# Windowed attention and two expert layers on one core: all filling matmuls ahead of the first scores, two more behind them, and a plan that books a slow start

## The chip, the cores and the metric

One core of a Trainium2 chip runs the whole program in one launch. The metric is device time in microseconds (us), the median of three runs. The engines are named as in the profile: PE is TensorE (PEld its weight loads), DVE is VectorE, ACT is ScalarE, POOL is GpSimd, SP is SyncE, which issues most DMAs.

## The reference

Attention over 4 batches and 8 heads, with 512 local and 32 global positions of 64 numbers each. A local query sees the 32 global keys and the local keys within 32 positions; a global query sees all keys. Two expert layers follow, on 2304 tokens of 512 numbers.

```python
# attention, per batch and head
out_g = softmax(scale * q_g @ k_all.T) @ v_all                    # 32 global queries
s_l   = concat([scale * q_l @ k_g.T, where(|i-j| <= 32, scale * q_l @ k_l.T, -1e9)])
out_l = softmax(s_l) @ concat([v_g, v_l])                         # 512 local queries
x = concat([out_g, out_l]) -> (2304, 512)
# first expert layer
h = x @ w_in                      # 512 -> 2048
x = (h * clip(h + 3, 0, 6) / 6) @ w_out
# second expert layer
h = maximum(maximum(x @ w1, x @ w2), x @ w3)    # 512 -> 768
return h @ w_out2
```

## The kernel before

**Stages.** Attention runs in 16 steps, one for each pair of heads of a batch (`pair`, line 440), with a step for the global queries of two pairs each (`globals_`, line 555). Beside it the first product of the first expert layer (`first`, line 680, matmuls of line 694) starts as soon as a batch of tokens and a decoded piece of `w_in` are there. The other products follow: the long one (line 858), the second layer's (line 982).

**One pair.** Its queries (`qr`), keys (`kr`) and values (`vr`) come by DMA from SP (lines 451, 454); each has three slots, so the load of a fourth pair waits until the first pair's slot is free. PE makes the scores (line 468, 64 small matmuls into two PSUM banks). DVE masks them and takes the row maxima (line 481), ACT the exponentials (line 487). PE turns the result over, once for each of the two heads (`flip`, line 511, four transposes each); DVE or ACT copies it out of PSUM (line 434, `pt<-s`); PE multiplies by the values (line 522), DVE norms (line 530), PE turns that over (line 537), ACT and DVE store it in two parts (lines 549 and 551). The global queries of two pairs have their own scores (line 575, twelve matmuls) and product with the values (line 619), which is the last reader of both pairs' values.

**The filling matmuls.** `fill` (line 417) writes a whole PSUM bank from a tile of ones, a matmul of 128 by 512. There are seven banks in which scores lie during the first pairs: five named `s`, and `bank` 6 and 7. Scores leave some columns unwritten, and the filling gives those a value. Before, six fillings stand ahead of the first scores, and the seventh (the fifth `s` bank) behind the first half of the first pair's scores. The first pair's scores are split in halves, since its queries and keys come in two loads each (the keys' by ACT's queue).

**What sets the order.** Every step is handed to a planner (`Plan.order`, line 141) with its engine, a booked duration, a due number and what it reads and writes. It walks through time by its own bookkeeping and gives each engine a fixed order of instructions. On the chip each engine then runs its list in that order, waiting where an input is not there yet. Booked durations steer only this order. For PE the planner also books twice the duration for 4 us behind a long idle time (`cold`, lines 234 to 237), and waits for the loading of PE's own instructions, 256 at a time (`border`). It begins as if PE were at full pace. A step with `rel` isn't taken up before that time; a smaller due number goes first.

Of the kernel before, what the change touches and what calls it, by code (L numbers as in the profile page):

```python
# [99 lines left out]
class Plan:  # L100
# [40 lines left out]
    def order(self):  # L141
# [4 lines left out]
        free, cand, out, pipe, port, form = {}, {}, [], 0.0, dict(DVE=0.0, POOL=0.0), "F"  # L146
# [9 lines left out]
        self.stalls = []  # L156
        count, border, there, loads, cold = 0, FIRST, 0.0, [], -1e9

# [36 lines left out]
        while len(out) < len(self.ops):  # L195
# [34 lines left out]
            if o.eng == "PE":  # L230
                if FORM.get(o.what, "F") != form:
                    form = FORM.get(o.what, "F")
                    us += TURN
                if t - free.get("PE", 0.0) > 2.0 and t > COLD:
                    cold = t + 4.0
                if t < cold:
                    us += min(us, (cold - t) / 2)
                count += o.ni
                if count > border:
                    at_ = t + us * (1 - (count - border) / o.ni)  # L240
                    wait_ = max(0.0, there - at_)
                    at_, us = at_ + wait_, us + wait_
                    if wait_ > 0.2:
                        self.stalls.append((round(at_, 1), round(wait_, 1)))
                    if wait_ > 2.0:
                        cold = at_ + 4.0
                    behind = max([p - at_ for i, p in loads if i <= at_] + [0.0])
                    there, border = at_ + 3.2 + min(4.0, 0.45 * behind), border + 256
# [29 lines left out]
FIRST = 193  # L278
COLD = 6.0
SPLIT = 2  # L280
# [14 lines left out]
def body(ctx, tc, q_n, k_n, v_r, w_in, w_o, w_3, w_4, out):  # L295
    nc = tc.nc
# [126 lines left out]

    full = [filled(bank) for bank in (*sbanks[:4], banks[6], banks[7])]

# [14 lines left out]
    def pair(b, pr, s0):  # L440
# [7 lines left out]
        for n, (t, src, cut, size) in enumerate(((Q, q_n, 256, NQ + SG), (K, k_n, 448, NK))):  # L448
            for i, (a, z) in enumerate(((0, cut), (cut, size)) if first_ else ((0, size),)):
                e, issue = ("ACT", nc.scalar) if first_ and n else ("SP", nc.sync)  # L450
                op(e, 0.45, lambda t=t, src=src, a=a, z=z, issue=issue: issue.dma_start(
                    out=t()[:, a:z], in_=src[b, pr][:, a:z]), s0 - 6 + i, w=[(t, i)] if first_ else [t],
                   kb=(z - a) / 2, rel=s0 - 14, what="qk"[n])
        op("SP", 0.5, lambda: nc.sync.dma_start(out=V(), in_=v_r[b, pr]), s0 - 3 + 5 * first_, w=[V], kb=1024, rel=s0 - 10, what="v")

        TB, NM, OB = [Buf(T["t"]) for _ in range(2)], Buf(T["nm"]), Buf(T["o"])
        for u, tiles in enumerate(((0, 1), (2, 3)) if first_ else (range(4),)):
# [3 lines left out]
            def scores(tiles=tiles, SB=SB):  # L461

                for i in tiles:
                    for c in range(4):
# [10 lines left out]
                      w=SB + [(t, "held") for t in TB], what="scores", ni=32 * len(tiles))  # L475
            if not full[6:]:
                full.append(filled(sbanks[4], [head]))
            for n, (hh, i) in enumerate((hh, i) for hh in range(2) for i in tiles):
# [749 lines left out]
```

## Time and profile before

| | us |
|---|---|
| median of three runs (719.79 to 720.88) | 719.81 |
| the profiled execution's own time | 722.88 |
| its span in the trace | 721.1 |
| PE busy | 700.2 |
| DVE, ACT, POOL busy | 533.1, 377.2, 125.9 |
| DMA, mean over the span | 200 GB/s |

The profiled execution took 3.07 us longer than the median, 1.78 us of it outside the span. Busy time of PE counts a matmul from its start to a modelled end, so a busy PE is not always a PE at its peak: the same matmuls take longer where the engine's clock is lower. The granted clock in the profile's rows (PEclk) reads 1.00 where no record of a lower one is there, and at the very start there is no record; there the durations tell.

### The profile page before, as it was taken

The numbers are of one execution on the slowest core, as the hardware profiler recorded it, in microseconds if no ns is written. First come the engines' busy times: TensorE is split into PE (matmuls) and PEld (weight loads), VectorE is DVE, ScalarE is ACT, GpSimd is POOL, SyncE is SP. The second block draws the span as 40 slices with busy tenths as digits, with TensorE's granted clock in tenths as the row PEclk, the third lists the DMA queues.
The fourth block names the chain that finished last, engine by engine and source line by source line (L and its number), as shares of the span: only waits on it lengthen the run. The fifth ranks groups of instructions, "written<-read, shape, count | busy, mean of one in ns | idle before, by whom it ended". The sixth has DMA issues, their size and how long they took to land.

```text
span 721.1 us, 16051 instructions
## 1 busy us (share of the span) xinstructions
PE 700.2 (97%) x6380; PEld 619.7 (86%) x6380; DVE 533.1 (74%) x1123; ACT 377.2 (52%) x802; POOL 125.9 (17%) x160
## 2 busy tenths in 40 slices
PE   8899998999999999999999999999999999999998
PEld 5677776778878999988899888898999999998998
DVE  4898886667864476699976679898978876576781
ACT  5788776754332244456564366754444435154452
POOL 2125543210001142103000000021211220021210
PEclk9999999999999999999999999999999999999999
DMA  8869888726863775686576588101363471366452
GB/s 340 306 236 343 299 315 309 275 90 193 316 234 161 283 279 193 225 258 194 150 227 188 151 263 272 66 0 59 125 213 113 151 236 57 103 202 210 139 159 88
DMA packets 73147, 144.57 MB, mean 200 GB/s; under 512 B 4976, under 2 KB 43632, under 8 KB 70000
## 3 DMA queue, kind: packets, MB, share of 16 engines
q1 hardware_dynamic: 72784, 143.13, 58.5%
q8 instruction: 50, 0.82, 0.5%
q10 hardware_dynamic: 288, 0.41, 0.2%
q14 instruction: 25, 0.20, 0.1%
HBM read 98.04 MB, written 45.48 MB: 199 GB/s over the span
## 4 chain that ended last, share of the span: by engine, by line
PE 70%; DMA 13%; DVE 9%; ACT 4%; issue 2%; POOL 1%; SPq 1%; DVEq 0%; ACTq 0%; POOLq 0%
PE bank L982 30%; PE bank L858 20%; PE bank L694 16%; DMA raw<-in_w_o_dram 3%; DMA raw<-in_w_in_dram 2%; DMA kr<-in_kn_dram 2%; DMA raw<-in_w_dram 2%; DMA rf<-hd 2%; DMA hd<-rf 1%; ACT t L487 1%; PE s L468 1%; PE s L511 1%; DVE rq L651 1%; DMA gsA<-rq 1%; DVE rr L676 1%
## 5 line engine op out<-in xcount | busy, mean ns | idle before, releaser
L694 PE MATMUL bank<-rx,rw 128*128 128x512 f32 (+1 forms) x960 | 199.8, 364 | 1.7 <-issue 1.0
L694 PEld LDWEIGHTS bank<-rx,rw 128*128 128x128 f32 x960 | 162.8, 189 | 25.4 <-issue 2.4
L858 PE MATMUL bank<-rr,rw 128*128 128x320 f32 (+2 forms) x912 | 155.2, 331 | 2.1 <-DVE rr L676 1.2
L858 PEld LDWEIGHTS bank<-rr,rw 128*128 128x128 f32 x912 | 140.3, 188 | 16.4 <-DVE rr L676 2.2
L982 PE MATMUL bank<-rw,rr 128*128 128x256 f32 (+2 forms) x648 | 100.1, 302 | 0.6 <-DVE rf L438 0.5
L982 PEld LDWEIGHTS bank<-rw,rr 128*128 128x128 f32 x648 | 90.6, 188 | 5.7 <-ACT rf L434 0.7
L676 DVE TENSOR_TENSOR rr<-fw,rr 128x1024 fp32r<-128x1024 f32 (+2 forms) x76 | 73.5, 973 | 22.6 <-ACT rr L781 21.8
L781 ACT CAST rr<-fw 128x1024 fp32r<-128x1024 f32 (+2 forms) x76 | 61.9, 819 | 52.9 <-PE bank L858 46.0
L704 ACT ACTIVATE rq<-bank,three 128x512 f32<-128x512 f32 (+1 forms) x60 | 37.7, 633 | 49.1 <-PE bank L694 41.6
L676 POOL TENSOR_TENSOR rf<-rf 128x256 f32<-128x256 f32 (+2 forms) x34 | 33.5, 998 | 141.1 <-DVE rf L651 39.6
L434 ACT COPY rf<-bank 128x512 f32<-128x512 f32 (+2 forms) x71 | 32.5, 466 | 48.9 <-PE bank L982 39.4
L706 DVE SCALAR_TENSOR_TENSOR rq<-rq,bank 128x512 f32<-128x512 f32 (+1 forms) x60 | 36.9, 619 | 28.1 <-ACT rq L704 27.8
L982 PE MATMUL bank<-rw,re 128*128 128x256 f32 (+2 forms) x369 | 54.3, 292 | 1.5 <-DVE rf L996 0.8
L982 PE MATMUL bank<-re,rr 128*128 128x512 f32 x222 | 55.0, 391 | 0.0
L487 ACT ACTIVATE t<-t,nm 128x128 f32<-128x128 f32 x128 | 49.7, 392 | 9.0 <-DVE nm L481 9.0
L676 POOL TENSOR_TENSOR rq<-rq 128x256 f32<-128x256 f32 (+2 forms) x43 | 35.9, 835 | 97.1 <-DVE rq L676 85.3
L982 PEld LDWEIGHTS bank<-rw,re 128*128 128x128 f32 x369 | 49.4, 188 | 3.3 <-DVE rf L996 1.0
L982 PEld LDWEIGHTS bank<-re,rr 128*128 128x128 f32 x222 | 40.7, 188 | 7.9
L1076 DVE TENSOR_TENSOR rf<-rf,bank 128x320 f32<-128x320 f32 (+2 forms) x72 | 37.0, 529 | 13.7 <-PE bank L982 12.5
L676 DVE TENSOR_TENSOR rf<-rf 128x256 f32<-128x256 f32 (+4 forms) x54 | 29.3, 573 | 7.0 <-DMA rf<-hd 6.8
L481 DVE CUSTOM_DVE_ANT_0 t<-s,mask 128x128 f32<-128x128 f32 x116 | 26.6, 285 | 9.4 <-PE s L468 9.4
L676 DVE TENSOR_TENSOR re<-rf,re 128x1024 fp32r<-128x1024 f32 (+4 forms) x20 | 26.5, 1331 | 3.5 <-ACT re L1159 3.5
(134 smaller groups left out, 970.4 us busy)
## 6 DMA issues: line engine op xcount, KB each, us to landing
vr<-in_v_dram SPq DMA_DIRECT2D x16, 1024.0 KB, 8.2
fw<-gsB SPq DMA_DIRECT2D x28, 512.0 KB, 4.5
raw<-in_w_dram SPq DMA_DIRECT2D x24, 512.0 KB, 4.2
fw<-gsC SPq DMA_DIRECT2D x28, 320.0 KB, 3.5
raw<-in_w_in_dram SPq DMA_DIRECT2D x16, 512.0 KB, 7.9
raw<-in_w_o_dram SPq DMA_DIRECT2D x16, 512.0 KB, 4.3
fw<-gsA SPq DMA_DIRECT2D x28, 256.0 KB, 2.8
gsB<-rq SPq DMA_DIRECT2D x6, 1024.0 KB, 4.6
```

The lines of the kernel that those rows point to most:

```text
L434: (nc.scalar.copy if eng == "ACT" else nc.vector.tensor_copy)(out=out, in_=in_)
L468: nc.tensor.matmul(SB[hh]()[QB * c:QB * c + QB, 128 * i + a:128 * i + z], lhsT=Q()[64 * hh:64 * hh + 64, QB * j:QB * j + QB], rhs=K()[64 * ...
L481: nc.vector.tensor_tensor_reduce(out=TB[hh]()[:, i], in0=SB[hh]()[:, 128 * i:128 * i + 128], in1=mask()[:, (i + 1) // 2 if i < 3 else 2], ...
L487: nc.scalar.activation(out=t, in_=t, func=ACTF.Exp, scale=-1.0, bias=NM()[:, 0, i, hh:hh + 1], accum_out=NM()[:, 1, i, hh:hh + 1])
L676: ENG[e].tensor_tensor(out=out, in0=a, in1=b, op=f)
L694: nc.tensor.matmul(ps()[:, 0:m], lhsT=w[:, i, k], rhs=xs(c)[:, j, k], start=(k == 0 and s == 0), stop=(k == KC - 1 and s == 2))
L704: op("ACT", us, lambda ps=ps, m=m, out=out: nc.scalar.activation(out=out(), in_=ps()[:, 0:m], func=ACTF.Relu, bias=three), -100, r=[ps], w ...
L706: op("DVE", us, lambda ps=ps, m=m, out=out: nc.vector.scalar_tensor_tensor(out=out(), in0=out(), scalar=6.0, in1=ps()[:, 0:m], op0=ALU.min ...
L781: op("ACT", act(n) + 0.01, lambda: nc.scalar.copy(out=out(0), in_=src()), due, r=r, w=[(w, "hi")], what=what + "_hi")
L858: nc.tensor.matmul(A[e]()[:, 0:n], lhsT=w[:, 2 * fp + f, u, e], rhs=r[:, v, f], start=(seed is None and fp + f + s == 0), stop=(fp == 3 an ...
L982: nc.tensor.matmul(bank()[:, 0:n], lhsT=w[:, u, k], rhs=r[:, v, k], start=(start and k + s == 0), stop=(k == K - 1 and s == 2), skip_group ...
L1076: op("DVE", dve(n), lambda q=q, src=src, mv=mv: nc.vector.tensor_tensor(out=mv(q)(), in0=mv(q)(), in1=src(), op=ALU.max), -200, r=[bank], ...
```

## The change

The seventh filling moves ahead of the first scores, beside the other six. A new step of two fillings (`WARMERS`) into the bank `o`, which the first product with the values will write later, stands behind the first pair's second half of scores. The planner begins with a time `WARM` of 8 us up to which it books PE's steps at up to twice their length, the fillings excepted; a long idle time books the slow stretch only from then on (before: from 6 us on). The loads of queries, keys and values of the first batch may be taken up by the planner from the start.

```diff
-        count, border, there, loads, cold = 0, FIRST, 0.0, [], -1e9
+        count, border, there, loads, cold = 0, FIRST, 0.0, [], WARM
...
-                if t - free.get("PE", 0.0) > 2.0 and t > COLD:
+                if t - free.get("PE", 0.0) > 2.0 and t > WARM:
                     cold = t + 4.0
-                if t < cold:
+                if t < cold and o.what != "fill":
                     us += min(us, (cold - t) / 2)
...
-COLD = 6.0
+WARM = 8.0
+WARMERS = 2
...
-    full = [filled(bank) for bank in (*sbanks[:4], banks[6], banks[7])]
+    full = [filled(bank) for bank in (*sbanks, banks[6], banks[7])]
...
-                   kb=(z - a) / 2, rel=s0 - 14, what="qk"[n])
-        op("SP", 0.5, lambda: nc.sync.dma_start(out=V(), in_=v_r[b, pr]), s0 - 3 + 5 * first_, w=[V], kb=1024, rel=s0 - 10, what="v")
+                   kb=(z - a) / 2, rel=s0 - 14 if b else 0, what="qk"[n])
+        op("SP", 0.5, lambda: nc.sync.dma_start(out=V(), in_=v_r[b, pr]), s0 - 3 + 5 * first_, w=[V], kb=1024, rel=s0 - 10 if b else 0, what="v")
...
-            if not full[6:]:
-                full.append(filled(sbanks[4], [head]))
+            if first_ and u:
+                op("PE", 0.43 * WARMERS, lambda: [fill(OB()) for _ in range(WARMERS)], -100, after=[head], w=[OB], what="fill", ni=2 * WARMERS)
```

The order moves on every engine through the whole of attention. Three places follow; the changed kernel's line numbers are one higher there (512 for 511, and so on).

First place: PE's list at the start of the program. `ones` is the tile of ones, `s_140` to `s_144` are the five score banks, `bank_129` and `bank_130` banks 6 and 7. Before:

```order
L418 MATMUL s_143<-ones 128x512
L418 LDWEIGHTS ones
L418 MATMUL bank_129<-ones 128x512
L418 LDWEIGHTS ones
L418 MATMUL bank_130<-ones 128x512
L468 MATMUL s_140<-kr,qr 32x96
...
L418 LDWEIGHTS ones
L418 MATMUL s_144<-ones 128x512
L468 MATMUL bank_129<-kr,qr 32x128
...
L468 MATMUL s_142<-kr,qr 32x96
```

Now:

```order
L419 MATMUL s_143<-ones 128x512
L419 LDWEIGHTS ones
L419 MATMUL s_144<-ones 128x512
L419 LDWEIGHTS ones
L419 MATMUL bank_129<-ones 128x512
L419 LDWEIGHTS ones
L419 MATMUL bank_130<-ones 128x512
L469 MATMUL s_140<-kr,qr 32x96
...
L419 MATMUL o<-ones 128x512
L419 LDWEIGHTS ones
L419 MATMUL o<-ones 128x512
L469 MATMUL s_142<-kr,qr 32x96
```

The filling of `s_144` has moved ahead of all scores, and two fillings of `o` stand between the first pair's scores and the second pair's (`s_142`).

Second place: PE's list behind the second pair's scores. `ident,t` are flips of the local pairs, `kr,qr 64x...` scores of the global queries, `vr,pt` products with the values, `ident,ox` the turning of the result, `ident,tg` flips of the global queries. Before:

```order
L511 MATMUL s_144<-ident,t 128x128 x4
L575 MATMUL s_140<-kr,qr 64x192 x4
L575 MATMUL s_141<-kr,qr 64x160 x2
L511 MATMUL s_142<-ident,t 128x128 x4
L511 MATMUL s_143<-ident,t 128x128 x4
L522 MATMUL o<-vr,pt 32x64 x32
L511 MATMUL s_144<-ident,t 128x128 x4
L537 MATMUL s_140<-ident,ox 128x128 x4
L606 MATMUL s_141<-ident,tg 128x128 x4
L522 MATMUL o<-vr,pt 32x64 x32
L606 MATMUL s_142<-ident,tg 96x128 x2
L537 MATMUL s_143<-ident,ox 128x128 x4
```

Now:

```order
L512 MATMUL s_144<-ident,t 128x128 x4
L512 MATMUL s_140<-ident,t 128x128 x4
L576 MATMUL s_141<-kr,qr 64x192 x4
L576 MATMUL s_142<-kr,qr 64x160 x2
L523 MATMUL o<-vr,pt 32x64 x32
L538 MATMUL s_143<-ident,ox 128x128 x4
L512 MATMUL s_144<-ident,t 128x128 x4
L512 MATMUL s_140<-ident,t 128x128 x4
L469 MATMUL bank_129<-kr,qr 32x96
...
L607 MATMUL s_141<-ident,tg 128x128 x4
L607 MATMUL s_142<-ident,tg 96x128 x2
L512 MATMUL s_143<-ident,t 128x128 x4
```

Both flips of the first pair now stand ahead of the global scores, and the third pair's scores (`bank_129`) ahead of the global flips and of the second pair's product with the values. Before, the global queries' product with the values of pairs one and two (line 619) stood right behind the third pair's scores; now it stands behind the fourth pair's scores and the third pair's product.

Third place: SP's list from its tenth row on. `raw` is a piece of `w_in` as loaded. Before:

```order
L451 DMA qr<-in_qn_dram 128x576
L451 DMA kr<-in_kn_dram 128x800
L663 DMA raw<-in_w_in_dram 128x4x256
L451 DMA qr<-in_qn_dram 128x576
L451 DMA kr<-in_kn_dram 128x800
L454 DMA vr<-in_v_dram 128x2048 x2
L663 DMA raw<-in_w_in_dram 128x4x256 x2
```

Now:

```order
L452 DMA qr<-in_qn_dram 128x576
L452 DMA kr<-in_kn_dram 128x800
L664 DMA raw<-in_w_in_dram 128x4x256
L452 DMA qr<-in_qn_dram 128x576
L452 DMA kr<-in_kn_dram 128x800
L664 DMA raw<-in_w_in_dram 128x4x256
L455 DMA vr<-in_v_dram 128x2048 x2
```

Up to these rows SP's list is the same; here the third piece of `w_in` moves ahead of the values of pairs four and five.

## Rows read from the trace of the kernel before

**Rows 1.** Stretches: length, then busy PE, PEld, DVE, ACT, POOL; PEclk, DMA, GB/s.

```profile
0.00:42.00 42.00, 35.90 (x850) 25.88 (x854) 29.31 (x136) 28.23 (x103) 8.07 (x29) 1.00 0.77 278
42.00:100.00 58.00, 55.31 (x1059) 43.71 (x1048) 49.17 (x181) 47.80 (x153) 27.17 (x36) 1.00 0.94 339
100.00:158.30 58.30, 54.00 (x1116) 43.13 (x1116) 40.37 (x157) 38.05 (x127) 19.41 (x30) 0.97 0.66 239
158.30:721.10 562.80, 554.94 (x3373) 506.99 (x3373) 414.28 (x652) 263.15 (x420) 71.28 (x65) 1.00 0.54 176
```

**Rows 2.** PE's timeline, first 20 us: start, length, line, tiles [idle before, releaser].

```profile
1.05 1.89 PE L418 MATMUL s<-ones 128*128 128x512 bf16 x4 [1.05 <-DVE ones L317]
...
4.10 1.11 PE L468 MATMUL s<-kr,qr 64*32 64x96 f32 x32 [0.30 <-DMA kr<-in_kn_dram]
...
5.68 1.09 PE L468 MATMUL bank<-kr,qr 64*32 64x128 f32 x32
7.71 1.95 PE L468 MATMUL s<-kr,qr 64*32 64x96 f32 x64 [0.94 <-DMA kr<-in_kn_dram]
9.59 1.11 PE L511 MATMUL s<-ident,t 128*128 128x128 f32 x4
10.63 2.08 PE L575 MATMUL s<-kr,qr 128*64 128x192 f32 x12
12.64 1.62 PE L511 MATMUL s<-ident,t 128*128 128x128 f32 x8
14.20 1.34 PE L522 MATMUL o<-vr,pt 128*32 128x64 f32 x64
...
19.98 0.87 PE L468 MATMUL bank<-kr,qr 64*32 64x96 f32 x43
```

**Rows 3.** PE's timeline later: the same kinds of steps.

```profile
22.43 1.14 PE L575 MATMUL s<-kr,qr 128*64 128x192 f32 x12
...
24.09 1.50 PE L468 MATMUL s<-kr,qr 64*32 64x96 f32 x64
...
34.49 1.10 PE L522 MATMUL o<-vr,pt 128*32 128x64 f32 x64
...
44.65 1.10 PE L468 MATMUL s<-kr,qr 64*32 64x96 f32 x64
...
141.78 1.04 PE L511 MATMUL s<-ident,t 128*128 128x128 f32 x8
...
158.36 41.62 PE L694 MATMUL bank<-rx,rw 128*128 128x512 f32 x195
```

**Rows 4.** SP's timeline: issues of the third and fourth pair's keys, and of values.

```profile
4.44 0.43 SPq L451 DMA_DIRECT2D kr<-in_kn_dram  x1
...
13.12 0.43 SPq L451 DMA_DIRECT2D kr<-in_kn_dram  x1
...
22.52 1.46 SPq L454 DMA_DIRECT2D vr<-in_v_dram  x2
```

**Rows 5.** DMA issues at 4.44 and 13.12: KB, us to landing; values' landings, 0 to 60.

```profile
kr<-in_kn_dram SPq DMA_DIRECT2D x1, 400.0 KB, 11.3
...
kr<-in_kn_dram SPq DMA_DIRECT2D x1, 400.0 KB, 8.4
...
DMA to landing us min/median/max: 4.8/8.0/13.4
```

**Rows 6.** Stretches early in attention, columns as in rows 1.

```profile
3.00:21.00 18.00, 15.79 (x344) 10.66 (x342) 10.03 (x50) 9.41 (x38) 2.00 (x10) 1.00 1.03 389
5.72:8.92 3.20, 2.26 (x83) 1.84 (x90) 1.54 (x14) 3.19 (x16) 0.00 (x0) 1.00 1.01 395
```

**Rows 7.** PE's timeline at its longest wait.

```profile
119.38 0.85 PE L537 MATMUL s<-ident,ox 128*128 128x128 f32 x4 [2.43 <-DVE nm L481]
119.89 5.14 PE L694 MATMUL bank<-rx,rw 128*128 128x512 f32 x15
```

**Rows 8.** The stretch behind that wait, columns as in rows 1.

```profile
119.59:123.00 3.41, 3.41 (x11) 2.76 (x10) 1.11 (x5) 1.53 (x6) 2.92 (x4) 0.50 0.56 221
```

## The prediction

> **What bounds the kernel now.** I read the stretches first, to see where PE, the busiest engine, is not fed. Behind 158.3 us it idles 562.80 - 554.94 = 7.9 us in 563; in the 158.3 us of attention it idles 6.1 + 2.7 + 4.3 = 13.1 us, nearly half of it in the first 42 [rows 1]. PE's work is the same before and after, but for two fillings, so time can come only from attention: from PE's idle time, and from time in which it runs slowly. What attention saves goes through to the end, because PE hardly waits behind it.
>
> Next I read PE's timeline at the start, for slow work. Four fillings of 512 columns take 1.89 us, some 0.43 each [rows 2]; that is 1.2 GHz, where the 195 matmuls of 512 columns at 158.36 take 41.62 us, 0.213 each, which is 2.4 GHz [rows 3]. The same holds up to about 13 us, read from like steps: the second pair's 64 scores take 1.95 us at 7.71 but 1.10 at 44.65; twelve global scores 2.08 at 10.63 but 1.14 at 22.43; eight flips 1.62 at 12.64 but 1.04 at 141.78 [rows 2, 3]. What PE did before the clock rose: it worked from 1.05, stood 0.30 us before 4.10 and 0.94 us before 7.71, both times for keys, and then ran on without a gap until the rise at some 13 us [rows 2].
>
> **The change part by part.** The sum is made against the profiled execution (722.88 us, span 721.1, 1.78 around it), which is 3.07 us longer than the median; the gain is then taken from the median.
>
> The seventh filling ahead. The first six end at about 1.05 + 6 x 0.43 = 3.6 us as the engine counts, and the first scores wait for keys until 4.10 [rows 2]. A seventh ends at 4.06: it hides in the 0.30 us wait. Bounds: 0 to 0.2 us later. The filling that it removes from between the two halves of the scores lets the second half start up to 0.43 us sooner. That is worth nothing: ACT, which takes the exponentials, is busy 3.19 of the 3.20 us from 5.72 to 8.92 [rows 6], and it started on the first half.
>
> The two fillings behind. They take 2 x 0.43 = 0.86 us and stand where PE waits 0.94 us for the second pair's keys [rows 2]; with the second half of scores ending up to 0.43 us sooner (5.68 + 1.09 = 6.77 before), they end at 7.2 to 7.6. The keys free the scores at 7.71. Cost 0; if that cover were gone, 0.86. Their bank `o` is written next by the first product with the values, some 4 us later on the same engine, so nothing new is waited for.
>
> The clock. With these fillings PE has no gap of over 0.1 us from 1.05 to 7.2, as long a stretch of work as the one from 7.71 that stood before the rise in the trace. I take the rise to come at about 7 us. The trace has no such start, so bounds: at worst the clock rises where it did, gain 0; at best everything from 7.71 on is at 2.4 GHz. That best is worked out of like rows: scores 1.95 - 1.10 = 0.85, four flips 1.11 - 1.04/2 = 0.59, twelve global scores 2.08 - 1.14 = 0.94, eight flips 1.62 - 1.04 = 0.58; together 2.96 us [rows 2, 3]. PE was without a gap over that stretch, so all of it lies on the path to the first product with the values at 14.20.
>
> The new order. Both flips of the first pair now stand ahead of the global scores (second place of the order). The flips end at about 7.71 + 1.10 + 1.04 = 9.9 us, their copies run beside the global scores (1.14 us, to 11.0), and the first product starts at about 11.0 in place of 14.20 [rows 2, 3]. The second pair's exponentials start some 0.9 us sooner, as its scores end at 8.8 in place of 9.66. The third pair's scores, now ahead of the global flips and the second product, then wait for little but their own keys (the second pair's flips stand ahead, and their exponentials began 0.9 us sooner). Those land at 4.44 + 11.3 = 15.7 us [rows 4, 5]; the scores started at 19.98 [rows 2]: 4.2 us sooner. The fourth pair's keys land at 13.12 + 8.4 = 21.5 [rows 4, 5], and will not land sooner, since the third piece of `w_in`, moved ahead of the values, comes behind them in SP's list. The fourth pair's scores started at 24.09 [rows 3], so at most 2.6 us is won there. Between 4.2 and 2.6 I take 3.4 us, the middle; 2.96 from the clock alone is next to it. Bounds for clock and order together: 0 to 4.2 us.
>
> Does it last? From 42 to 100 us PE idles 2.7 us in 58 [rows 1]: there it is bound by its own work, and a start 3.4 us sooner shifts it all if it is fed. DVE and ACT are busy 49.2 and 47.8 of those 58 us, so they follow, with some 15% to spare. DMA is at 0.94 there, the least spare of all, but from 100 to 158 at 0.66.
>
> The rest of attention is reshuffled; PE's single waits move. The largest price that rows show is the one at 119.38: 2.43 us idle, and then 3.41 us at a granted clock of 0.50, 1.2 GHz, which costs half of it, 1.7 us [rows 7, 8]: 4.1 us in all. It may go, or another may come: -4.1 to +4.1, taken as 0, since the order does not tell.
>
> The earlier take-up of the first batch's loads costs nothing by itself: SP's list is the same up to the third piece of `w_in`.
>
> Sum: 0 (fillings) - 3.4 (clock and order) + 0 (later waits) = -3.4 us; 722.88 becomes 719.5, and the median 719.81 becomes 716.4.
>
> **The transfers.** From 3 to 21 us all 16 DMA engines are busy (share 1.03, 389 GB/s), and 400 KB of keys issued at 4.44 took 11.3 us to land [rows 4 to 6]. So what is issued sooner lands no sooner while that lasts. The Trainium skill (DMA: Bandwidth & Descriptors, "Issuing engines are not separate DMA queues") says that transfers of all issuing engines run on the same 16 DMA engines and interleave; the trace agrees, with 11.3 us for 400 KB. By that rule PE would only wait where it worked slowly before; what this gives is the second rival.
>
> **The rivals.**
>
> First, the clock does not rise sooner: the fillings change nothing but the order. Then the second pair's scores take 1.95 us again, both flips another 2.1, and the first product comes at about 13.0 in place of 14.20, the third pair's scores at about 17: 1 to 3 us sooner, of which the fourth pair's keys and the flips before them leave about 1. Time 718.8. For it: PE had been working most of the time from 1.05 on and the clock stayed down until 13 us. Against it: there were two gaps then.
>
> Second, the transfers set the pace. PE reaches the fourth and fifth pair sooner and stands there for keys and values, and the 3.4 us melt to 0 to 1 us: 719.5. For it: a DMA share of 1.03 to 21 us and of 0.94 from 42 to 100 [rows 1, 6]. Against it: over the first 42 us it is 0.77, so there is room in between.
>
> Third, slower: the values of pairs four and five come late. Their loads were issued at 22.52, as soon as the global product with the values (line 619) had freed the slots [rows 4]. In the new order that product stands behind the fourth pair's scores (not before 21.5), the global scores, the third pair's product and itself: 21.5 + 1.1 + 1.1 + 1.1 + 0.9 = 25.7 us at the least, so the issue is 3 to 4 us later than before. Values land 4.8 to 13.4 us behind the issue, 8.0 in the middle [rows 5]: at 30.5 to 39. The fourth pair's product stood at 34.49 [rows 3]. Up to a landing of 34.5, 8.8 us behind the issue, nothing is lost against before; beyond it PE stands, with everything in its list behind. At 37 us that is 2.5 us, too long for the clock to stay up if it goes as at 119.38 (2.43 us): 1.7 more [rows 7, 8], and the early gain is gone with it: 719.8 + 2.5 + 1.7 = 724.0, or 722.3 if the clock stays up. I take 722.8; the most would be at 39: some 726.
>
> Fourth, better: the wait at 119.38 and the slow stretch behind it do not come again, in another order of steps: 716.4 - 4.1 = 712.3. For it: it is the one such wait of the whole trace. Against: the later order is as tight.
>
> **How the numbers follow.** Forecast 716.4, chance 0.47, by itself from 715 to 718.2. Clock not sooner, 718.8: 0.09. Transfers, 719.5: 0.12. Slower, 722.8: 0.14. Better, 712.3: 0.18. A measurement of this kernel tells about 0.2% (1.44 us) from no change, so faster is below 718.4, slower above 721.3. Faster: 0.47 + 0.18, and a third of the first rival, 0.03: 0.68. Same: 0.06 + 0.12 = 0.18. Slower: 0.14. The range runs from 712.0 to 721.0: it takes in the better case's middle and the two small ones, and leaves out the slower one and some of what lies below 712.
>
> **What would show it.** Right: the second pair's 64 scores take about 1.1 us and no longer 1.95; the next flips 0.52 for four; the first product with the values starts at about 11, the third pair's scores at about 16, the fourth pair's product no later than 34.5, and the last step of attention on PE some 3 us before 158.3. Wrong: the scores at 7.7 still take 1.95 us; a gap of over 2 us before the fourth pair's product; a new stretch at a clock of 0.50; or as much idle time before 158 us as the 13.1 of now.

## The result, and the profile after

The changed kernel takes 725.80 us (median of four runs, 725.05 to 726.85); the kernel before, run beside it, 719.91 (719.79 to 720.88): ratio 1.0080, 95% interval 1.0062 to 1.0097. It is slower by 0.8%; 716.4 was forecast, with 721.0 as the upper end. On another occasion (e5 below) the changed kernel took 721.18 against 718.60: 1.0042 (1.0011 to 1.0072). The sign is the same there, and the size about half.

The profiled execution took 725.05 us, with a span of 723.3. The stretches of the kernel after, cut where those of [rows 1] were cut, and once more where attention now ends (columns as there):

```profile
0.00:42.00 42.00, 34.68 (x856) 25.11 (x857) 27.04 (x132) 30.65 (x108) 9.37 (x30) 0.96 0.85 308
42.00:100.00 58.00, 53.71 (x1018) 42.14 (x1018) 47.63 (x177) 45.46 (x140) 29.94 (x36) 0.97 0.90 311
100.00:158.30 58.30, 54.48 (x1010) 43.55 (x1010) 36.48 (x149) 39.85 (x138) 17.34 (x29) 0.94 0.66 245
158.30:164.50 6.20, 6.20 (x138) 4.92 (x136) 3.23 (x8) 2.26 (x6) 0.19 (x1) 1.00 0.02 5
164.50:723.30 558.80, 552.39 (x3365) 505.30 (x3363) 414.21 (x648) 263.77 (x422) 70.07 (x65) 1.00 0.54 178
```

PE idles 7.3 + 4.3 + 3.8 = 15.4 us up to 158.3, where it idled 13.1 [rows 1]. And the granted clock, which showed a loss in the third stretch alone, now shows one in all three (the slow start of before had no record and reads 1.00). Next PE's timeline at the start, after (start, length, line, operation, tiles, count, and in brackets the idle time before and its releaser), against [rows 2]:

```profile
1.05 2.31 PE L419 MATMUL s<-ones 128*128 128x512 bf16 x5 [1.05 <-DVE ones L318]
...
5.92 0.61 PE L419 MATMUL o<-ones 128*128 128x512 bf16 x2
7.42 1.10 PE L469 MATMUL s<-kr,qr 64*32 64x96 f32 x64 [0.90 <-DMA kr<-in_kn_dram]
8.45 1.09 PE L512 MATMUL s<-ident,t 128*128 128x128 f32 x8
9.47 1.16 PE L576 MATMUL s<-kr,qr 128*64 128x192 f32 x12
10.56 1.38 PE L523 MATMUL o<-vr,pt 128*32 128x64 f32 x64
13.54 0.66 PE L538 MATMUL s<-ident,ox 128*128 128x128 f32 x4 [1.60 <-DVE nm L503]
14.03 1.04 PE L512 MATMUL s<-ident,t 128*128 128x128 f32 x8
15.00 1.10 PE L469 MATMUL bank<-kr,qr 64*32 64x96 f32 x64
...
18.47 0.80 PE L523 MATMUL o<-vr,pt 128*32 128x64 f32 x41
21.37 0.54 PE L523 MATMUL o<-vr,pt 128*32 128x64 f32 x23 [2.10 <-issue]
```

The start went as forecast, and more. The second pair's scores take 1.10 us, eight flips 1.09, the global scores 1.16: all at 2.4 GHz. The first product with the values starts at 10.56 in place of 14.20, the third pair's scores at 15.00 in place of 19.98. (Whether the fillings raised the clock is another matter: see e2.) Then PE stops in the middle of one product, after 41 of its 64 matmuls, for 2.10 us, and "issue" says that no semaphore held it. When it goes on, at 21.37, it has 348 matmuls behind it (the counts of the whole list add up to that); the kernel before began its 349th, too, at 21.11. The whole lead is gone at this one place.

Three more such stops follow, and attention's last step; below them the stretches behind the four stops (columns as in the first table):

```profile
33.40 1.10 PE L523 MATMUL o<-vr,pt 128*32 128x64 f32 x64
...
43.00 1.57 PE L576 MATMUL s<-kr,qr 128*64 128x192 f32 x8 [2.19 <-issue]
...
100.94 0.40 PE L695 MATMUL bank<-rx,rw 128*128 128x512 f32 x1 [2.66 <-issue]
...
144.41 0.38 PE L523 MATMUL o<-vr,pt 128*32 128x64 f32 x10 [2.39 <-issue]
...
164.47 0.27 PE L628 MATMUL s<-ident,gx 128*128 128x128 f32 x1
```

```profile
22.73:26.14 3.41, 3.41 (x73) 2.47 (x51) 3.11 (x17) 2.51 (x7) 1.28 (x1) 0.50 0.24 50
43.21:46.62 3.41, 3.41 (x15) 2.33 (x14) 0.48 (x1) 0.43 (x1) 0.00 (x0) 0.50 1.14 380
101.23:104.64 3.41, 3.41 (x12) 2.84 (x11) 1.03 (x2) 1.36 (x5) 0.00 (x0) 0.50 0.61 222
145.61:149.02 3.41, 3.41 (x32) 2.68 (x37) 0.85 (x6) 1.69 (x7) 0.08 (x1) 0.50 0.41 159
```

Each of the four stops is followed by 3.41 us at a clock of 0.50, 1.2 GHz, in which PE is busy throughout and gets half as far: 1.7 us lost each time. The kernel before had one such pair [rows 7, 8].

**What PE stands for.** The page's first part counts PE's instructions, its third the DMA queues (packets, MB, share of 16 engines); here both of the kernel after, and then queues 1 and 8 in the window from 18.7 to 20.0 us:

```profile
PE 701.5 (97%) x6382; PEld 621.0 (86%) x6382; DVE 528.6 (73%) x1112; ACT 382.0 (53%) x812; POOL 126.9 (18%) x161
...
q8 instruction: 50, 0.82, 0.5%
```

```profile
q1 hardware_dynamic: 396, 0.46, 102.5%
q8 instruction: 1, 0.02, 5.4%
```

Queue 8 carries 50 packets of 0.82/50 MB = 16 KB; 2 x 6382 matmuls and weight loads over 50 are 255 instructions. So it brings PE's own program, 256 instructions at a time. Its packet of this window ran from 18.80 to 19.92 us, on DMA engines that were full of data, and PE went on 1.45 us behind its end. The other three stops stand in the same way 1.3 to 1.4 us behind a packet (40.62 to 41.63, 98.55 to 99.56, 142.12 to 143.00). So does the wait of 1.60 at 13.54 (11.15 to 12.20), but the profile puts that one down to DVE, and rightly: its step turns `ox`, which DVE ended at 13.41 only.

```profile
12.72 0.69 DVE L531 TENSOR_TENSOR ox<-o,nm 128x512 f32<-128x512 f32 x1
```

In the kernel before, the stop of [rows 7] stands 1.3 us behind a packet of 117.10 to 118.06, and the packet of 18.75 to 19.86 cost 0.26 us.

A count settles which waits are for blocks. PE's stops fall at its 349th, 857th, 1875th, 2257th and 2638th matmul after, and at the 349th, 603rd, 1494th, 1621st, 1875th, 2257th and 2639th before: some 127 matmuls apart, or a multiple of that, and 127 matmuls with their weight loads are 254 of a block's 256 instructions. The cuts between blocks lie at the same counts in both lists; the new order puts other steps there.

When a packet comes depends on the data. Of the first 21 packets of both traces (42), 28 met DMA engines that were at 0.9 or more in the 2 us behind the matmul at the previous cut; these packets started 0.9 to 6.1 us behind that matmul, 3.7 in the middle. Four met engines under 0.5 and started 0.2 to 1.1 us behind it. The other ten lie in between. Here one stretch of 2 us of each kind, of before (packet at 38.90, 0.31 us behind) and of after (packet at 18.80, 5.26 behind):

```profile
38.59:40.59 2.00, 2.00 (x22) 1.58 (x24) 2.00 (x6) 2.00 (x5) 0.20 (x1) 1.00 0.03 8
13.54:15.54 2.00, 2.00 (x54) 1.83 (x60) 0.85 (x2) 1.61 (x5) 0.19 (x1) 1.00 0.98 405
```

**The ledger.** Up to attention's end the trace after is late by 164.47 - 158.27 = 6.2 us, less nine matmuls of the first expert product that it had done more (nine at 0.213): 4.3. From the parts: 15.4 - 13.1 = 2.3 more idle time, and three more slow stretches, 5.1, less the 2.96 that the fast start saves: 4.4. Behind attention 2.1 us come back, 1.5 of them as idle time (6.4 us, before 7.9). That leaves the 2.2 us between the two spans; the profiled run of before was the longest of its kind and that of after the shortest, hence 5.9 between the medians. The mean clock of the four runs, 0.989, against 0.997 in the profiled run of before would be 0.008 x 722 = 5.8 us; that this is near 5.9 proves nothing, since the 0.997 leaves out before's slow start, and the ledger has idle time in it besides.

### The profile page after: what moved, and what is told of

Its sections match the earlier page's. It is cut to its first block, busy times and chain, and to the rows that moved or that the text cites. A ratio compares the mean times of both kernels' runs of the same rounds, so it can differ in the third digit from the quotient of the medians.

```text
span 723.3 us, 16047 instructions
## 1 busy us (share of the span) xinstructions
PE 701.5 (97%) x6382; PEld 621.0 (86%) x6382; DVE 528.6 (73%) x1112; ACT 382.0 (53%) x812; POOL 126.9 (18%) x161
## 4 chain that ended last, share of the span: by engine, by line
PE 80%; DMA 8%; DVE 5%; ACT 3%; issue 3%; SPq 0%; POOL 0%; DVEq 0%; ACTq 0%
PE bank L983 30%; PE bank L695 22%; PE bank L859 20%; DMA rf<-hd 2%; PE o L523 2%; PE s L469 2%; PE s L512 2%; DMA raw<-in_w_dram 2%; DMA raw<-in_w_o_dram 1%; DMA raw<-in_w_in_dram 1%; ACT t L488 1%; DMA kr<-in_kn_dram 1%; PE s L538 1%; DVE rr L677 1%; PE s L576 1%
## 5 line engine op out<-in xcount | busy, mean ns | idle before, releaser
L677 DVE TENSOR_TENSOR rr<-fw,rr 128x1024 fp32r<-128x1024 f32 (+2 forms) x76 | 71.6, 948 | 22.6 <-ACT rr L782 22.0
L435 ACT COPY rf<-bank 128x256 f32<-128x256 f32 (+2 forms) x72 | 32.8, 464 | 46.7 <-PE bank L983 37.0
L677 POOL TENSOR_TENSOR rq<-rq 128x256 f32<-128x256 f32 (+2 forms) x45 | 39.6, 879 | 99.5 <-DVE rq L677 82.2
L1077 DVE TENSOR_TENSOR rf<-rf,bank 128x320 f32<-128x320 f32 (+2 forms) x72 | 37.0, 529 | 14.4 <-PE bank L983 13.1
```

The lines of the kernel that those rows point to most:

```text
L435: (nc.scalar.copy if eng == "ACT" else nc.vector.tensor_copy)(out=out, in_=in_)
L677: ENG[e].tensor_tensor(out=out, in0=a, in1=b, op=f)
L1077: op("DVE", dve(n), lambda q=q, src=src, mv=mv: nc.vector.tensor_tensor(out=mv(q)(), in0=mv(q)(), in1=src(), op=ALU.max), -200, r=[bank], ...
```

## The experiments

The theory formed from the two traces: the added time is waits for PE's own blocks of instructions, and the slow clock behind them. A block that lies behind data doesn't come sooner because PE is sooner. Rivals: the order of the steps (PE waiting for its inputs), the fillings themselves, the earlier transfers. A letter in a quoted expectation means what the expectation says beside it. They ran on four chips (e1 to e4, e5 to e8, e9 to e12, e13 and e14), each beside the kernel before on its own, so across these groups ratios are compared and not medians. "Lost to the clock" is (1 - mean granted clock of all timed runs) x 720 us; "waits" is the sum, in the profiled attention, of PE's waits of over 0.2 us that end 1.1 to 1.7 us behind a block. That rule goes by time alone. By the count above, a few of these waits stand at no cut and ended with an input: 1.56 us of e6 (28.44), 2.38 of e7 (76.20), 1.79 of e8 (21.50). At the 222nd matmul (12 to 17 us), which is a cut, an input was in some runs as late as the block. So the column is rather too high.

| run | median us | before beside it | ratio (95%) | lost to the clock, and before | waits, us |
|---|---|---|---|---|---|
| e1 fillings only | 721.58 | 718.90 | 1.0047 (1.0021 to 1.0072) | 3.0, 1.9 | 11.1 |
| e2 order only | 720.43 | 718.90 | 1.0017 (0.9991 to 1.0044) | 4.9, 1.9 | 10.1 |
| e3 after, cuts moved | 722.97 | 718.90 | 1.0067 (1.0041 to 1.0094) | 5.0, 1.9 | 10.9 |
| e4 after, half the values | 716.88 | 718.90 | 0.9955 (0.9929 to 0.9982) | 2.1, 1.9 | 8.3 |
| e5 after again | 721.18 | 718.60 | 1.0042 (1.0011 to 1.0072) | 4.7, 2.0 | 11.8 |
| e6 before, cuts moved | 722.41 | 718.60 | 1.0055 (1.0027 to 1.0082) | 4.5, 2.0 | 9.3 |
| e7 after, late loads | 717.56 | 718.60 | 0.9984 (0.9961 to 1.0008) | 3.0, 2.0 | 9.5 |
| e8 plan with longer blocks | 729.17 | 718.60 | 1.0139 (1.0095 to 1.0183) | 3.4, 2.0 | 6.9 |
| e9 early loads only | 721.88 | 719.05 | 1.0031 (1.0009 to 1.0053) | 4.4, 2.4 | 8.7 |
| e10 late loads, no new filling | 717.32 | 719.05 | 0.9967 (0.9948 to 0.9987) | 3.4, 2.4 | 6.3 |
| e11 loads 12 and 8 ahead | 727.30 | 719.05 | 1.0098 (1.0070 to 1.0127) | 5.0, 2.4 | 11.1 |
| e12 loads 10 and 6 ahead | 724.67 | 719.05 | 1.0070 (1.0047 to 1.0094) | 3.5, 2.4 | 6.3 |
| e13 after, an eighth of the values | 710.59 | 719.01 | 0.9886 (0.9862 to 0.9911) | 1.1, 2.9 | 5.0 |
| e14 before, an eighth of the values | 713.08 | 719.01 | 0.9924 (0.9895 to 0.9952) | 2.4, 2.9 | 2.0 |

**e1: the fillings in the order of before.**

```diff
-    full = [filled(bank) for bank in (*sbanks[:4], banks[6], banks[7])]
+    full = [filled(bank) for bank in (*sbanks[:4], banks[6])]
+    full.append(op("PE", 0.43, lambda: (fill(sbanks[4]), fill(banks[7])), -100, rel=0.4, what="fill", ni=2))
...
+                if first_ and u:
+                    fill(OB())
+                    fill(OB())
```

> The order of before on every engine, with the new fillings alone: the seventh ahead of the first scores, two into the bank o behind the first pair's scores. Three theories. Blocks: PE reads its instructions in blocks of 256, a block's load takes about 3 us on quiet DMA queues and 6 to 9 us on full ones, and what costs in the changed kernel is that the new order runs through whole blocks of small matmuls in 2 to 3 us just when the queues are full (waits of 2.10, 2.19, 2.66 and 2.39 us, each with 3.41 us at 1.2 GHz behind it). By it this kernel, whose blocks are cut as before but for 4 instructions, is not slowed: 717 to 720.5 us, at most two stretches at the lower clock behind the rise, and the rise at about 6 us. Early clock: what costs is the earlier clock itself, since PE then runs into the full DMA queues of the first 40 us; by it this kernel shows the loss: 723 to 727. Order: the new order is worse by itself, whatever blocks do; by it 717 to 720, with the waits of before.

Slower by 0.47%, with the same order of work but for the fillings, and cuts that come four instructions sooner in it. PE's timeline at the place of [rows 2]'s last row:

```profile
18.77 0.86 PE L469 MATMUL bank<-kr,qr 64*32 64x96 f32 x41
21.89 0.62 PE L469 MATMUL bank<-kr,qr 64*32 64x128 f32 x23 [2.27 <-issue]
```

The third pair's scores start 1.2 us sooner than in [rows 2], and PE stands in them for 2.27 us. The block ran from 19.33 to 20.43, not sooner than before. A lead of 1.2 us over the profiled execution of before became a deficit of 0.8 and a slow stretch. That the early clock is what costs isn't shown by this run; the next ones say why.

**e2: the order of after without the two fillings.**

```diff
-                op("PE", 0.43 * WARMERS, lambda: [fill(OB()) for _ in range(WARMERS)], -100, after=[head], w=[OB], what="fill", ni=2 * WARMERS)
+                op("PE", 0.43 * WARMERS, lambda: None, -100, after=[head], w=[OB], what="fill", ni=2 * WARMERS)
```

> The changed kernel's order on every engine, without the two fillings behind the first pair's scores (they are left out, and nothing else). Blocks theory: the blocks are cut as in the changed kernel but for 4 instructions, so the waits for instructions near 43, 101 and 144 us stay, each of over 2 us, with a slow stretch behind; 724 to 728 us. Early-clock theory: PE has a gap ahead of the second pair's scores again, the clock rises at 10 to 14 us, and the loss goes: 719 to 721.5. Order theory: as the changed kernel, 724 to 728, and it would not matter where the blocks are cut.

Unclear by itself (0.9991 to 1.0044). The clock rose early all the same (the second pair's scores took 1.10 us), so the run doesn't separate the order from the clock; the stop at the second block was there (2.12 us at 21.72).

It rose early with the fillings of before, too. In e9 (below), whose first steps on PE are those of before, fillings included, the clock was up as early, and the second pair's scores took 1.10 us behind a wait of 1.18:

```profile
5.11 0.61 PE L418 MATMUL s<-ones 128*128 128x512 bf16 x1
...
7.54 1.10 PE L468 MATMUL s<-kr,qr 64*32 64x96 f32 x64 [1.18 <-DMA kr<-in_kn_dram]
...
11.86 1.21 PE L522 MATMUL o<-vr,pt 128*32 128x64 f32 x62
```

So these traces don't show that the new fillings raise the clock; why it rose late in the profiled execution of before stays open. That execution was 2.97 us longer than the median of 719.91, and its slow start was worth 2.96. That before mostly starts fast would fit, but it is not shown: the start has no record in the timed runs' clock.

**e3 and e6: the cuts between the blocks moved.** 56 small matmuls behind the fillings, or in the kernel before behind the second scores, push every later cut by 112 instructions.

```diff
+    def small_one(bank, i):
+        c = i % 4
+        nc.tensor.matmul(bank[QB * c:QB * c + QB, 0:8], lhsT=ones[:, 0:QB], rhs=ones[:, 0:8], start=True, stop=True,
+                         tile_position=(0, QB * c))
...
+                    for i in range(56):
+                        small_one(OB(), i)
```

> The changed kernel with 56 small matmuls more (128 rows, 32 by 8, some 16 to 30 ns each) behind the two fillings, in PE's wait for the second pair's keys: they compute nothing that is used, and they move all later cuts between PE's instruction blocks by 112 instructions, in the same order of work. Blocks theory: the waits of over 2 us near 21, 43, 101 and 144 us do not stay where they are; they go or come at other steps, and the time moves by 2 us or more, up or down; counted from the order, more blocks are now nothing but small matmuls, so rather up, 727 to 732. Order theory and early-clock theory: nothing but the 0.3 us by which the matmuls outlast the wait, 725 to 727, with the same waits at the same steps.

> The kernel before, same order of work, with 56 small matmuls behind the first pair's second scores (some 1.5 to 2 us of work of their own, in a stretch where PE runs up to its data), so that each later 256-instruction block is cut 112 instructions earlier in the work. Theory A: the waits behind block loads stand at other steps and have other lengths, their sum in the attention anywhere from 4 to 13 us against 6.4 before, and the time follows that sum and the granted clock: 715 to 727 us, not tied to 720. Rival C (the order of the steps alone sets the time): 719 to 721.5 us, the same order having the same waits.

e3: the stops moved, to 12.00, 17.89, 25.02 and 112.50 us; the time stayed near after's, below what was expected. e6 is the sharper one: the order of before, only cut elsewhere, is 0.55% slower, with three slow stretches in its profile. The small matmuls' own 0.63 us aren't what it pays: they lie in the wait for keys, and the second pair's scores start at 7.67, before at 7.71. The same order doesn't have the same waits. PE's timeline of e3 and then of e6, at a stop each, and e3's stretch around it:

```profile
107.69 0.85 PE L528 MATMUL o<-vr,pt 128*32 128x64 f32 x47
112.50 0.69 PE L528 MATMUL o<-vr,pt 128*32 128x64 f32 x17 [3.97 <-issue]
```

```profile
111.20:118.00 6.80, 5.50 (x39) 3.93 (x39) 3.78 (x6) 2.98 (x12) 0.73 (x1) 0.50 0.99 364
```

```profile
15.88 1.02 PE L530 MATMUL o<-vr,pt 128*32 128x64 f32 x57
19.07 0.32 PE L530 MATMUL o<-vr,pt 128*32 128x64 f32 x7 [2.17 <-issue]
```

Both stops cut a product of 64 small matmuls in two: such a run uses up a block in 2 to 3 us (scores and a product together are 256 instructions).

**e4: half of each pair's values loaded.**

```diff
-out=V(), in_=v_r[b, pr]
+out=V()[:, 0], in_=v_r[b, pr][:, 0]
...
-rhs=V()[:, hh, 4 * i + c]
+rhs=V()[:, 0, 4 * i + c]
```

> The changed kernel, with the values of only one of the two heads of each pair loaded (512 in place of 1024 KB for each pair) and used for both; so the output is another, and the DMA queues carry 8 MB less of the 42 or so that they move during attention. Order and blocks as in the changed kernel. Blocks theory: the instruction loads wait less behind data, and of the five waits of over 1.5 us at most two are left; 715 to 720 us. Order theory: PE waits for its own steps, and the time falls by 2 us at the most, to 723.5 to 726. Early-clock theory: some of the loss of the first 40 us goes, the rest stays: 721 to 724.

The global queries' product reads the same half. Faster by 0.45% than before, with smaller waits; but with less to load, less of everything waits, so e13 and e14 repeat it as a pair.

**e5: the changed kernel again.**

> The changed kernel unaltered, on the chip of these experiments. Theory A (the added time is waits of PE for its own 16 KB instruction blocks, and the stretches at the clock's lower level behind waits of over 2 us): about 725 us here too, mean granted clock near 0.990 (before: 0.997), three or four stretches at 0.50 in the first 160 us, and runs with a lower clock are the longer ones. Rival B (the first trace and the first timing were chance, the kernels are equal): within 1 us of before, clock as before.

2.6 us slower between the medians; 2.7 us more lost to the clock. The waits are those of the first trace, at 14.1, 22.3, 44.6, 102.4, 124.6 and 145.2 us: they belong to the program and not to chance.

**e7, e9, e10: the early loads apart.** e7 is the changed kernel with the diff below; e9 is the kernel before with only the early loads; e10 is e7 without the two fillings (as e2).

```diff
-                   kb=(z - a) / 2, rel=s0 - 14 if b else 0, what="qk"[n])
+                   kb=(z - a) / 2, rel=s0 - 14, what="qk"[n])
...
-kb=1024, rel=s0 - 10 if b else 0, what="v")
+kb=1024, rel=s0 - 10, what="v")
```

> The changed kernel with one part undone: the transfers of the first batch's pairs are again not booked before 14 (query and key) or 10 units (values) ahead of their pair's due time, instead of from 0 on. The fillings, the booked first steps and the clock rule stay. Theory D (the earlier transfers put more data in flight, and the blocks of instructions wait behind it): waits behind block loads in the first 60 us shrink from 1.60 + 2.10 + 2.19 to under 3 us in sum, the stretches at 0.50 there go, time 718 to 721. Theory A without D (where the cuts fall matters, not how early the transfers are): the order is another one from the third pair on, waits of 8 to 12 us in sum all the same, 722 to 727.

> The kernel before with one part of the change alone: the first batch's transfers may be booked from 0 on (no fillings added, first steps booked as before). Theory D (early transfers put more data in flight, and PE's blocks of instructions wait behind it): the first 60 us hold waits behind block loads of over 5 us in sum (before: 1.6) and one or two stretches at 0.50, time 721 to 724 us. Theory A without D (where the cuts fall in the work decides, whatever moved them): any sum between 5 and 12 us for the whole attention, the time in step with the granted clock, 716 to 725 us. Rival C (order alone, data on time earlier is better): 716 to 719.

> The changed kernel with late loads, and without the two fillings behind the second scores (the order is that of the kernel with late loads). Theory A: 4 instructions fewer ahead of every cut and one pause more or less at the start move the waits little; 715.5 to 719.5 us, waits at 14, 22 and 76 us within 0.7 us of those with the fillings. Theory E (the fillings themselves cost, as the kernel with the fillings alone suggested at +0.47%): 713 to 715.5 us.

e7 gives back the loss (0.9984, where the changed kernel beside it, e5, is at 1.0042), the early loads alone cost 0.31% (e9), and e2 against e10 points the same way. But not as the expectation of e9 had it: its first 60 us hold 3.2 us of waits and no slow stretch, and its largest stop comes late:

```profile
114.45 0.50 PE L694 MATMUL bank<-rx,rw 128*128 128x512 f32 x1
118.94 2.29 PE L694 MATMUL bank<-rx,rw 128*128 128x512 f32 x5 [4.00 <-issue]
```

So the early loads cost through another order, with other steps at the cuts; that more data in flight lengthens the early waits is not shown by it. e10 is faster than before by 0.33% (0.9948 to 0.9987); the changed kernel, on another chip, was slower than its own before (e5), so by the ratios e10 beats both. Its stretches, and its one slow stretch in attention:

```profile
0.00:42.00 42.00, 34.11 (x891) 25.73 (x895) 28.98 (x141) 30.12 (x112) 8.90 (x29) 0.96 0.83 299
42.00:100.00 58.00, 55.89 (x1123) 44.38 (x1112) 51.35 (x182) 49.44 (x152) 29.77 (x39) 1.00 0.94 338
...
8.29:11.70 3.41, 3.41 (x72) 2.74 (x55) 1.21 (x11) 1.82 (x8) 0.20 (x1) 0.50 0.98 404
```

The new fillings aren't what it gains by; e7, which has them, is at 0.9984, with an interval that overlaps e10's.

**e8, e11, e12: plans that should avoid the waits.** e8 is e7 with a block booked at 4.6 us and 0.6 of the data in flight (at most 5), where the plan has 3.2, 0.45 and 4. e11 and e12 book loads 12 and 8, or 10 and 6 units ahead in place of e7's 14 and 10.

```diff
-                    there, border = at_ + 3.2 + min(4.0, 0.45 * behind), border + 256
+                    there, border = at_ + 4.6 + min(5.0, 0.6 * behind), border + 256
```

> As the kernel with late loads, and the plan books a block of instructions as there 4.6 us + 0.6 of the data in flight (at most 5) behind the last cut, instead of 3.2 + 0.45 (at most 4), which is what the two traces show of block loads. Theory A: an order drawn up with the true wait avoids the waits of over 2 us: at most one stretch at 0.50 in the attention, 713 to 718 us, faster than both kernels. Rival C: the longer booked waits only delay the other bookings, 719 to 726.

> The changed kernel with every transfer booked at the earliest 12 (query and key) or 8 units (values) ahead of its pair's due time. Theory D: less data in flight than with 14 and 10, waits behind block loads under 8 us in sum, granted clock 0.997 or more, 714 to 717 us. Theory A without D: another order with other cuts, 8 to 12 us of waits, 716 to 723. Rival F (transfers set the pace): later loads make PE wait for data, 720 to 726.

> The same with 10 and 6 units. Theory D: still fewer bytes in flight, block loads of under 6 us throughout, waits under 7 us in sum, unless PE waits for data; 714 to 718 us. Theory A without D: 716 to 723. Rival F: 722 to 728, with gaps on PE ended by a transfer of queries, keys or values.

All three are slower, e8 by 1.4%. It does what it was meant to (waits of 6.9 us, none over 1.8), and pays more elsewhere: PE idles 18.4 us in its first 160, where after idles 15.4. e11 idles 18.2 in them, and 20.64 to 27.46 and 146.93 to 150.35 us are at 0.50. e12 idles 14.6 with three slow stretches' worth, which doesn't make up its 5.6 us; that is left open.

**e13 and e14: both orders with light transfers.** An eighth of the values, in the kernel after and in the kernel before; they differ by the change alone.

```diff
-out=V(), in_=v_r[b, pr]
+out=V()[:, 0, 0:4], in_=v_r[b, pr][:, 0, 0:4]
...
-rhs=V()[:, hh, 4 * i + c]
+rhs=V()[:, 0, c]
```

> The changed kernel, with an eighth of every pair's values loaded (128 KB in place of 1024; the products all read that eighth, so the output is another one; the number and shape of matmuls are unchanged). Theory A (blocks of instructions wait behind data): the second block of instructions lands by about 17 us in place of 19.9, the wait of 2.10 us at 21.37 is gone or under 0.7, and this kernel is 2 to 5 us faster than its partner with the order of before. Rival G (the block comes late for a reason of its own): it lands at 19 to 20.5 us as in all runs so far, the wait stays near 2 us, and the two partners are within 1 us, or this one is the slower as with all values.

> The kernel before with the same eighth of the values. Theory A: few waits behind block loads in the attention (under 3 us in sum), clock 0.998 or more, and 2 to 5 us slower than its partner with the order of after, as it starts later and neither has waits to lose the lead in. Rival G: within 1 us of the partner or faster.

The global queries' product reads the same eighth. Here the change makes the kernel faster: 710.59 against 713.08, 2.5 us, with ranges that overlap by 0.7 us only (709.11 to 712.06 and 711.35 to 714.89). PE's timeline at the second block, of e13 and then of e14, and their second stretches:

```profile
14.37 1.04 PE L512 MATMUL s<-ident,t 128*128 128x128 f32 x8
...
18.81 0.80 PE L523 MATMUL o<-vr,pt 128*32 128x64 f32 x41
20.23 0.54 PE L523 MATMUL o<-vr,pt 128*32 128x64 f32 x23 [0.61 <-issue]
```

```profile
20.53 0.87 PE L468 MATMUL bank<-kr,qr 64*32 64x96 f32 x43
21.93 0.58 PE L468 MATMUL bank<-kr,qr 64*32 64x128 f32 x21 [0.53 <-issue]
```

```profile
42.00:100.00 58.00, 57.27 (x1102) 45.81 (x1105) 50.04 (x188) 50.92 (x157) 32.35 (x42) 1.00 0.74 245
```

```profile
42.00:100.00 58.00, 55.78 (x1111) 44.81 (x1109) 50.22 (x185) 49.13 (x157) 27.00 (x36) 1.00 0.77 250
```

With light transfers the block follows PE. PE begins its 222nd matmul, the one at the cut before (349 less 127), at 13.88 in e13 and at 15.86 in e14; the second block's packet starts at 17.86 and at 19.64: 4.0 and 3.8 us behind. With all values the 222nd begins at 13.54 after and 15.31 before, and the packet starts at 18.80 and 18.75: PE is 1.8 us sooner, its instructions are not. The DMA engines aren't idle in e13 and e14 either (0.96 and 1.04 up to the packet), so the share alone doesn't say how long it waits. The packet came only 1 us sooner than in after, not the 3 that were expected, and a wait of 0.61 remains; but the lead lasts (1.66 us at the 354th matmul, 20.31 against 21.97), and no slow stretch comes in e13 before 133 us. Up to 1.3 of the 2.5 us may be clock: e14 loses 2.4 us to it and e13 1.1, and e14's trace has a slow stretch from 7.33 to 14.16.

## Why the prediction was wrong

The terms, one by one. **The fillings** cost nothing at their place, as forecast: the keys still end the wait ahead of the second pair's scores. **The clock and the order** gave 3.6 us at the first product with the values and 5.0 at the third pair's scores: as a number, -3.4 was right up to there. Its reason is not shown. With before's first steps, e9 has its first product at 11.86, so 2.3 of the 3.6 us came there without the new fillings and the new order; the prediction took the late rise of one execution for the kernel's own.

**"The rest of attention is reshuffled; PE's single waits move", taken as 0 with bounds of 4.1**, is the step that failed. It was sized by the one wait of [rows 7, 8], as if there were one to win or lose. By the count of matmuls, the trace held seven waits at cuts between blocks of instructions, 5.8 us together, only one of them over 2 us; the other order has five, 9.6 us, and behind four of them the clock fell. Against before the term measured 2.3 us of idle time and 5.1 of slow clock: 7.4, outside its bounds.

**"The earlier take-up of the first batch's loads costs nothing by itself: SP's list is the same up to the third piece of `w_in`"** is where the reshuffling came from. SP's list was compared, and PE's order further on was not: with the take-up alone e9 is 2.8 us slower than before, and without it e7 is 3.6 us faster than the changed kernel beside it.

**"So a start 3.4 us sooner shifts it all if it is fed"** failed for the same reason. DVE, ACT and DMA were weighed as the feeders; PE's own instructions, which come by DMA too, were not, although the plan has a rule for them and [rows 7] showed their wait, put down to DVE. The lead was lost at 21.4 us, and from 42 to 100 us PE idled 4.3 us in place of 2.7.

**The rivals.** "Transfers set the pace" had the mechanism: a transfer that lands no sooner because PE is sooner. It named keys and values, where it is the program, and it foresaw only the loss of the lead, not the slow clock behind each stop. The Trainium skill's rule cited with it (DMA: Bandwidth & Descriptors, "Issuing engines are not separate DMA queues") speaks of transfers that engines issue. For PE's own packets the trace has to speak: that of 18.80 runs in a window in which queue 1 alone takes 102.5% of the engines. The slower rival, values of pairs four and five too late, did not come: the fourth pair's product starts at 33.40 with no wait, before the 34.5 that was named as a sign of being right. The list of what would show it wrong did point at the right thing: "a new stretch at a clock of 0.50" (four in place of one) and idle time above 13.1 us (15.4).

Shown: that PE stands at the cuts between blocks and goes on behind a packet (every trace), that moving the cuts moves the stops (e3, e6), that the loss goes when the early loads are undone (e5, e7), that the lead lasts where transfers are light (e13 against e14). Argued only: which event makes the hardware ask for a block. Open: what raises the clock early, why e1 is slower, and why e12 is as slow as it is.

## What to carry to other kernels

A lead in an engine's list is worth something only if all that feeds the engine can come sooner, its own instructions among them: on a kernel of many small matmuls look for "issue" waits in the middle of a step and lay the instruction queue's packets beside them. A new order is also a new set of cuts, so in a kernel bound by PE any reordering carries some microseconds of either sign (here -2 to +11 among plans of the same work); bound that term by the sum of all such waits, each with the slow clock that may follow, not by the largest. The mean granted clock of the timed runs tells only a part: e5 loses 2.7 us more to it than before beside it, with 2.6 between the medians, but e2 loses 3.0 more and is 1.5 slower, and e8 1.4 more and 10.6 slower. And a slow start seen in one profiled execution need not be the kernel's usual one: look at a second trace with the same first steps before booking a gain on it.

## What the runs showed of the hardware

- PE's instructions came as packets of 16 KB on a DMA queue of their own. PE went on 1.2 to 1.6 us behind the end of the packet it stood for.
- A packet started 0.2 to 1.1 us behind the matmul at the previous cut where the DMA engines were under 0.5 in the 2 us behind it, and 0.9 to 6.1 us behind it where they were at 0.9 or more (before and after, 4 and 28 packets). For the second packet it was 3.4 us before, 5.3 after, 5.2 in e1 (14.14 to 19.33), 3.8 and 4.0 with light values.
- In the trace after, the clock stood at 0.50 for 3.41 us behind each stop of 2.10, 2.19, 2.39 and 2.66 us, and not behind the 1.60 at 13.54. Around e3's 3.97 it was 6.83 us (from 111.18), around e9's 4.00 it was 3.41. Behind e2's 2.12 (21.72) and e10's 2.09 (101.97) the clock stayed up.
